# Three re-orderings in the dense half of an attention, MoE and MLP kernel: operand sums, an early load, and who copies the token numbers

## The chip, the cores and the metric

One core of a Trainium2 chip runs the whole program. The metric is the device time of one execution in microseconds; the kernel before takes 1034.37 us (median of 3 runs, 1034.16 to 1036.52). The engines are named as the profile names them: PE (matmul), DVE (vector), ACT (scalar), POOL (GpSimd), SP (issues most DMAs).

## The reference

```python
def _attn_ref(q, k, v):                        # 4 x 12 x 448 x 64
    scores = scale * np.matmul(q, k.transpose(0, 1, 3, 2)) - np.log(S)
    return np.matmul(1.0 / (1.0 + np.exp(-scores)), v)

def _moe_ref(x, w_gate, w1, w2):               # 1792 tokens x 768, 8 experts, F = 1024
    logits = x @ w_gate
    expert_idx = np.argmax(logits, axis=1)     # gate_w: softmax probability of that expert
    for e in range(E):
        mask = expert_idx == e
        h = np.maximum(x[mask] @ w1[e], 0.0)
        out[mask] = gate_w[mask, None] * (h @ w2[e])

def _moe2_ref(x, w_in, w_out):                 # 768 -> 2048 -> 768
    h = np.maximum(x @ w_in, 0.0)
    return h * h @ w_out
```

The output is `_moe2_ref(_moe_ref(attention))`, 1792 x 768 in float32.

## The kernel before

Three stages follow each other on one core. Attention fills about the first quarter of the span. Then the routed experts: tokens are sorted by expert and packed into 15 slots of 128 rows; each slot gathers its rows, multiplies through two weight matrices and writes its result rows to the DRAM table `y_d` (L587), whose 769th column is the token's number. Four "quarter" pieces of 32 rows take the overflow and are copied into `y_d` by POOL after the last slot (L803). A branch (L783) on the routing result skips six further slots.

The dense MLP, where the change lies, runs over two blocks of tokens: block 0 has two halves of 4 tiles of 128 tokens, block 1 two halves of 3 (`blocks`, P = 4 and 3). The two halves and the two halves of each weight matrix are combined in a Strassen-like scheme of seven products, so operands and weights have sums and differences formed on DVE.

- Every float32 matrix is split into a high and a low part: ACT copies it to the narrower type (`sh`, `wrh`), DVE subtracts to get the rest (`sl`, `wrl`). Each product is then three matmuls.
- `load_y` loads one tile of 128 rows of `y_d` to SBUF (`yn`, two buffers); `trans_y` has POOL copy its 769th column to `idx2` (L460, the row numbers for the final scatter), PE transpose it, and ACT and DVE split it.
- Layer 1: `layer1(c, h)` handles weight chunk c and token half h with 36 matmuls (two accumulations of 18); `steps` sets the order of the 16 calls of a block. Weight chunks pass through a ring of three; `advance` stages the next one.
- The weights of layer 2 are converted and summed by `narrow`. For five of the chunks (11 to 15) this is done in pieces between the matmuls of layer 1 in block 0: `rest()` is called four times per `layer1` and does one piece each time (40 pieces, of which some are empty). Sources lie in `rawb[2]`, results in `rawb[3]`; each chunk's result goes to the DRAM table `t_d` and comes back as `raw` when its turn comes (L416).
- Layer 2: seven products `o`, each of four steps `q`; g = 4*o + q counts the 28 steps of a block. A step has 6*P matmuls of 384 columns. `split_s(g + 2)` prepares the operand of the step two ahead. Products 0 to 6 read the operand blocks a11, a12, s2, s2 (after `a22 - s2`), a22, a11 (after `a11 + s2`), a12 (after `a12 - s2`), in this order. At the end of a product `evac` adds the PSUM tiles into the result (L914 on DVE, or ACT); products 2, 3 and 4 go on in the same PSUM tiles, so the first matmul of a product waits for the evacuation before it. After products 5 and 6 `scatter` writes result rows to `out` by an indirect DMA on POOL (L827).
- While block 0 is in steps g = 20 to 25 the six tiles of block 1 are loaded, transposed and split, one after each step.

Instructions of each engine run in the order in which the code was written (a manual schedule up to the last scatters), so an instruction that waits holds everything behind it on its engine. SP issues its DMAs in order too.

Of the kernel before, what the change touches and what calls it, by code (L numbers as in the profile page):

```python
# [40 lines left out]
QB = 2  # L41
# [20 lines left out]
def moe_kernel(ctx: ExitStack, tc: tile.TileContext, qk, v, wg, wm, w2, out):  # L62
# [363 lines left out]
    todo = [(n, k) for n in range(PRE, 16) for k in range(1, 9)]  # L426

    def rest():
        if not todo:
            return  # L430
        n, step = todo.pop(0)
        if step < 7:
            narrow(n, step, rawb[2], rawb[3], None)
        if step == 4 and n < 15:
            narrow(n + 1, 0, rawb[2], None, None)
        if step == 6:
            ready[0] = n + 1
            load_next()

    def load_y(bi, h, t, pool, bufs, tag="yn"):  # L440
        yn = pool.tile([128, DM + 1], F32, tag=tag, name=f"yn_{bi}_{h}_{t}", bufs=bufs)
        r_ = (blocks[bi][0] + h * blocks[bi][1] + t) * 128
        nc.sync.dma_start(out=yn, in_=y_d[r_:r_ + 128, :DM + 1])
        return yn
# [11 lines left out]
    def trans_y(bi, h, t, yn, yT, pool, tags):  # L456
        P = blocks[bi][1]
        n, yh, yl = yT
        c = blocks[bi][0] + h * P + t
        nc.gpsimd.tensor_copy(idx2[:, c:c + 1], yn[:, DM:].bitcast(U32))  # L460
        per = 3 if n == 3 else 4
# [20 lines left out]
    with ExitStack() as mctx:  # L482
# [250 lines left out]
        for s in range(NBASE):  # L733
            last = s == NBASE - 1
            up, down, fin = make_slot(s, *xs.pop(s), lambda c: (mh[c], ml[c]))
            if s + 2 < NBASE:
                regs(s + 2)
                if s > 0:
                    row0(s + 2)
                xg[s + 2] = gather(s + 2)  # L740
            for c in range(4):
                up(c)
# [40 lines left out]
        with tc.If(more < NT):  # L783
            for s in range(NBASE, NSLOT):
# [4 lines left out]
                def fresh(c, s=s, e_=e_):  # L789
                    wr = raw[6]  # L790
                    nc.gpsimd.dma_start(out=wr, in_=wm[ds(e_, 1), :, c].rearrange("a p n -> (a p) n"))
                    split_w(wr, mh[4 + c % 4], ml[4 + c % 4])
                    return mh[4 + c % 4], ml[4 + c % 4]
# [39 lines left out]
    load_next()  # L833
    yns = {t: load_y(0, 1, t, tp, 2) for t in range(2)}
    for bi, (t0, P) in enumerate(blocks):
# [7 lines left out]
        def layer1(c, h):  # L843
            w = used[0] + (0 if (c, h) not in ((1, 0), (7, 1)) or bi else 1)
            wc, wcl = wrh[w % RING], wrl[w % RING]
# [37 lines left out]
        if bi == 0:  # L883
            steps = [(0, 0), (1, 0), (0, 1), (1, 1)] + [(c, h) for c in range(2, 6) for h in range(2)] + [(6, 1), (7, 1), (6, 0), (7, 0)]
        else:
            steps = [(c, h) for c in range(8) for h in range(2)]
        seen = {}
        for c, h in steps:
            layer1(c, h)
            if bi == 0 and c < 2 and h == 0:  # L890
                for t in (2 * c, 2 * c + 1):
                    trans_y(0, 1, t, yns.pop(t), yT[1], ps_q, ("pq", "pq"))
                    if t + 2 < P:
                        yns[t + 2] = load_y(0, 1, t + 2, tp, 2)
            seen[c] = seen.get(c, 0) + 1
# [24 lines left out]
        def adds(o, q):  # L920
            a11, a12, s2, a22 = (hid[b, q][:, :2 * N] for b in range(4))
            if o == 1:
                V.tensor_tensor(a12, a12, s2, op=ALU.subtract)
            elif o == 2:
                V.tensor_tensor(a11, a11, s2, op=ALU.add)

        def third(g):
            o, q = divmod(g, 4)
            if o == 3:
                s2, a22 = hid[2, q][:, :2 * N], hid[3, q][:, :2 * N]  # L930
                V.tensor_tensor(s2, a22, s2, op=ALU.subtract)  # L931
# [6 lines left out]
        for o in range(len(PRODS)):  # L938
            for q in range(4):
                g = 4 * o + q  # L940
                third(g + 2)
                split_s(g + 2)
# [29 lines left out]
    order.close()  # L972
    prev = None
    for p in range(P):
        st = scatter(t0 + p, obs[0][p])
        if prev is not None:
            tc.declare_no_dep(st.ins, prev.ins, reason="every scatter writes rows of its own")
        prev = st

# [47 lines left out]
```

## Time and profile before

| | |
|---|---|
| median of 3 runs | 1034.37 us |
| the profiled execution | 1032.5 us, its span (first to last instruction) 1030.4 us |
| PE busy | 957.6 us, 93% of the span |
| DVE busy | 637.5 us, 62% |
| ACT busy | 566.3 us, 55% |
| POOL busy | 150.5 us, 15% |
| mean granted clock of PE | 0.967 of full speed |
| dense stage, from the first dense matmul to the end | 541.75 to 1030.4 us of the span |

The profile was taken on one execution, so its 1032.5 us is what durations add up to; it lies 1.9 us under the median of the runs. PE is the engine that sets the span, and its idle stretches are the time that can be had without taking work away. A stretch that PE passes at a granted clock near 0.5 (1.2 instead of 2.4 GHz) takes about twice its time at full speed.

### The profile page before, as it was taken

What the parts mean: (1) busy time and instruction counts of PE and PEld (TensorE: products, weight loads), DVE (VectorE), ACT (ScalarE), POOL (GpSimd) and SP (SyncE); (2) the same over time, 40 slices, a digit from 0 to 9 for tenths busy, and PEclk for the clock granted to TensorE, in tenths of its full rate; (3) what the DMA queues carried; (4) which work ended last, traced back from release to release, by engine and by line L of the source; (5) the groups of instructions that cost most, each with busy time, mean ns of one, the idle gap of its engine ahead of it and who ended that gap; (6) DMA issues with size and microseconds to landing.
All of it is one profiled execution on the core that took longest, in us unless ns stands there. A gap on an engine that the chain in (4) does not pass through costs nothing.

```text
span 1030.4 us, 15058 instructions
## 1 busy us (share of the span) xinstructions
PE 957.6 (93%) x5870; PEld 807.2 (78%) x5870; DVE 637.5 (62%) x657; ACT 566.3 (55%) x674; POOL 150.5 (15%) x134
## 2 busy tenths in 40 slices
PE   7999999288999999999996999999899699999896
PEld 3555555176888888888885788889899699999896
DVE  2877788688767767777754576236767322227762
ACT  4666666266777777777762444355344234446440
POOL 0000000237214323233211000000000110000002
PEclk9999999678999999999998999999999899999998
DMA  8789886633678594396555454303234431113202
GB/s 280 257 294 320 286 297 224 250 124 103 250 266 319 190 383 140 118 326 225 183 185 196 168 200 174 132 31 104 81 123 138 138 123 62 62 62 123 93 31 92
DMA packets 51261, 184.32 MB, mean 179 GB/s; under 512 B 7856, under 2 KB 18736, under 8 KB 49136
## 3 DMA queue, kind: packets, MB, share of 16 engines
q1 hardware_dynamic: 33136, 146.48, 40.4%
q0 software_dynamic: 6832, 31.07, 7.7%
q10 hardware_dynamic: 11216, 5.75, 2.2%
q8 instruction: 47, 0.77, 0.3%
q14 instruction: 30, 0.25, 0.1%
HBM read 209.62 MB, written 36.97 MB: 239 GB/s over the span
## 4 chain that ended last, share of the span: by engine, by line
PE 68%; DMA 4%; DVE 3%; issue 2%; ACT 2%; POOL 1%; POOLq 0%; SPq 0%; DVEq 0%; ACTq 0%
PE pp L854 7%; PE pp L853 7%; PE pp L855 7%; PE pq L958 6%; PE pq L959 6%; PE pq L960 6%; PE ph L523 4%; PE py L523 4%; PE py L525 4%; PE py L524 4%; PE ph L524 4%; PE ph L525 3%; DMA qraw<-in_wm 2%; PE qb L650 1%; DVE wl L397 1%
## 5 line engine op out<-in xcount | busy, mean ns | idle before, releaser
L397 DVE TENSOR_TENSOR wl<-raw,wh 128x1536 fp32r<-128x1536 f32 x103 | 202.9, 1978 | 70.6 <-ACT wh L396 67.9
L396 ACT ACTIVATE wh<-raw 128x1536 fp32r<-128x1536 f32 x120 | 177.8, 1488 | 14.7 <-DMA raw<-in_wm 7.0
L185 ACT ACTIVATE a<-sc,bias_s 128x896 f32<-128x896 f32 x96 | 82.5, 910 | 36.1 <-PE sc L181 36.0
L859 ACT ACTIVATE r<-pp 128x512 f32<-128x512 f32 (+1 forms) x64 | 34.8, 544 | 121.1 <-PE pp L855 121.1
L958 PE MATMUL pq<-wrh,sh 128*128 128x384 f32 x264 | 90.2, 342 | 4.2 <-DVE raw L914 4.2
L959 PE MATMUL pq<-wrl,sh 128*128 128x384 f32 x264 | 89.8, 340 | 0.0
L960 PE MATMUL pq<-wrh,sl 128*128 128x384 f32 x264 | 89.8, 340 | 0.0
L524 PE MATMUL py<-wl,hh 128*128 128x384 f32 x240 | 82.9, 346 | 5.2 <-POOL wl L397 5.2
L523 PE MATMUL py<-wh,hh 128*128 128x384 f32 x240 | 86.5, 360 | 0.0
L525 PE MATMUL py<-wh,hl 128*128 128x384 f32 x240 | 83.1, 346 | 2.4 <-DVE hl L553 2.4
L397 POOL TENSOR_TENSOR wl<-raw,wh 128x1536 fp32r<-128x1536 f32 x17 | 59.9, 3530 | 158.0 <-ACT wh L396 158.0
L397 DVE TENSOR_TENSOR wrl<-raw,wrh 128x1536 fp32r<-128x1536 f32 x30 | 52.8, 1759 | 38.4 <-ACT wrh L396 38.4
L523 PE MATMUL ph<-wh,xh 128*128 128x512 f32 x180 | 76.0, 422 | 0.3 <-ACT xh L509 0.3
L867 DVE TENSOR_TENSOR h<-h,h 128x512 f32<-128x512 f32 (+1 forms) x16 | 10.0, 625 | 102.0 <-ACT h L862 102.0
L879 ACT ACTIVATE sh<-h 128x1024 fp32r<-128x1024 f32 (+1 forms) x56 | 51.7, 944 | 38.1 <-DVE h L931 26.9
L524 PE MATMUL ph<-wl,xh 128*128 128x512 f32 x180 | 72.1, 401 | 0.0
L525 PE MATMUL ph<-wh,xl 128*128 128x512 f32 x180 | 72.0, 400 | 0.0
L880 DVE TENSOR_TENSOR sl<-h,sh 128x1024 fp32r<-128x1024 f32 (+1 forms) x56 | 59.8, 1087 | 17.8 <-ACT sh L879 17.7
L396 ACT ACTIVATE wrh<-raw 128x1536 fp32r<-128x1536 f32 x30 | 44.6, 1485 | 44.3 <-PE pq L960 36.1
L191 PE MATMUL po<-a,qkv 128*64 128x448 f32 x288 | 64.7, 556 | 0.0
L958 PEld LDWEIGHTS pq<-wrh,sh 128*128 128x128 f32 x264 | 50.6, 192 | 4.5 <-ACT rh L396 4.5
L853 PE MATMUL pp<-why,wrh 128*128 128x512 f32 (+1 forms) x132 | 49.6, 376 | 2.5 <-PEq L783 2.5
(232 smaller groups left out, 2169.7 us busy)
## 6 DMA issues: line engine op xcount, KB each, us to landing
raw<-in_wm SPq DMA_DIRECT2D x120, 768.0 KB
qraw<-in_wm SPq DMA_DIRECT2D x32, 768.0 KB
raw<-t_d SPq DMA_DIRECT2D x28, 768.0 KB
cs<-in_w SPq DMA_DIRECT2D x11, 1536.0 KB
raw<-w_d SPq DMA_DIRECT2D x16, 768.0 KB
qkv<-in_qk SPq DMA_DIRECT2D x23, 480.0 KB
raw<-in_w SPq DMA_DIRECT2D x5, 1536.0 KB
t_d<-raw POOLq DMA_DIRECT2D x5, 1536.0 KB, 7.1
```

What stands on the lines that cost most here:

```text
L185: nc.scalar.activation(a[:, :n], ps[:, :n, :S], AF.Sigmoid, bias=bias_s, scale=1.0 / math.sqrt(D))
L396: nc.scalar.activation(h, src, AF.Copy)
L397: (nc.gpsimd if pool else nc.vector).tensor_tensor(l, src, f32(h), op=ALU.subtract)
L523: nc.tensor.matmul(ps, lh, rh, start=first, stop=False)
L524: nc.tensor.matmul(ps, lh, rl, start=False, stop=False)
L525: nc.tensor.matmul(ps, ll, rh, start=False, stop=last)
L853: nc.tensor.matmul(pp[:, :N], lh, rh, start=(k == 0), stop=False)
L854: nc.tensor.matmul(pp[:, :N], lh, rl, start=False, stop=False)
L855: nc.tensor.matmul(pp[:, :N], ll, rh, start=False, stop=(k == KD - 1))
L958: nc.tensor.matmul(po[p][:, :DH], lh, wc[:, w0:w0 + DH], start=(q == 0 and kk == 0 and o in (0, 2, 5)), stop=False, **fl)
L959: nc.tensor.matmul(po[p][:, :DH], lh, wcl[:, w0:w0 + DH], start=False, stop=False, **fl)
L960: nc.tensor.matmul(po[p][:, :DH], ll, wc[:, w0:w0 + DH], start=False, stop=(q == 3 and kk == 1), **fl)
```

## The change

Three edits, and one on the branch that is not taken.

1. Operand sums. `a11 + s2` moves from the steps of product 2 to those of product 0; `a22 - s2` moves from `third(g + 2)`, called directly ahead of the split that reads it, to the steps of product 2, two steps ahead of that split. Each step of products 0, 1 and 2 then has one such sum, placed behind the step's split.
2. The second token half of block 0. Three of its four tiles are loaded in the last expert slot into `rawb[3]` (the result buffer of the weight conversion), the fourth after the branch as before. The pieces of the weight conversion are held for the first eight calls of `rest`. The order of `layer1` calls becomes three chunks of the first half, then three of the second.
3. The token numbers are copied to `idx2` by DVE instead of POOL. And the last three scatters are declared independent of each other in all pairs, not of the neighbour alone.

```diff
+    held = [8]
+
     def rest():
-        if not todo:
+        held[0] -= 1
+        if not todo or held[0] >= 0:
             return
...
     def load_y(bi, h, t, pool, bufs, tag="yn"):
-        yn = pool.tile([128, DM + 1], F32, tag=tag, name=f"yn_{bi}_{h}_{t}", bufs=bufs)
+        yn = pool if bufs is None else pool.tile([128, DM + 1], F32, tag=tag, name=f"yn_{bi}_{h}_{t}", bufs=bufs)
...
-        nc.gpsimd.tensor_copy(idx2[:, c:c + 1], yn[:, DM:].bitcast(U32))
+        nc.vector.tensor_copy(idx2[:, c:c + 1], yn[:, DM:].bitcast(U32))
...
+            if last:
+                yns = {t: load_y(0, 1, t, rawb[3][:, t * (DM + 1):(t + 1) * (DM + 1)], None) for t in range(3)}
...
                 def fresh(c, s=s, e_=e_):
-                    wr = raw[6]
+                    wr = mp.tile([128, CH], F32, tag="qraw", name=f"fr{s}_{c}", bufs=QB)
...
-    yns = {t: load_y(0, 1, t, tp, 2) for t in range(2)}
+    yns[3] = load_y(0, 1, 3, tp, 2)
...
-            w = used[0] + (0 if (c, h) not in ((1, 0), (7, 1)) or bi else 1)
+            w = bi * NW + c
...
-            steps = [(0, 0), (1, 0), (0, 1), (1, 1)] + [(c, h) for c in range(2, 6) for h in range(2)] + [(6, 1), (7, 1), (6, 0), (7, 0)]
+            steps = [(c, h) for h in range(2) for c in range(3)] + [(c, h) for c in range(3, 6) for h in range(2)] + [(6, 1), (7, 1), (6, 0), (7, 0)]
...
                     trans_y(0, 1, t, yns.pop(t), yT[1], ps_q, ("pq", "pq"))
-                    if t + 2 < P:
-                        yns[t + 2] = load_y(0, 1, t + 2, tp, 2)
...
         def adds(o, q):
             a11, a12, s2, a22 = (hid[b, q][:, :2 * N] for b in range(4))
-            if o == 1:
+            if o == 0:
+                V.tensor_tensor(a11, a11, s2, op=ALU.add)
+            elif o == 1:
                 V.tensor_tensor(a12, a12, s2, op=ALU.subtract)
             elif o == 2:
-                V.tensor_tensor(a11, a11, s2, op=ALU.add)
-
-        def third(g):
-            o, q = divmod(g, 4)
-            if o == 3:
-                s2, a22 = hid[2, q][:, :2 * N], hid[3, q][:, :2 * N]
                 V.tensor_tensor(s2, a22, s2, op=ALU.subtract)
...
-                third(g + 2)
                 split_s(g + 2)
...
-    prev = None
+    sent = []
     for p in range(P):
         st = scatter(t0 + p, obs[0][p])
-        if prev is not None:
-            tc.declare_no_dep(st.ins, prev.ins, reason="every scatter writes rows of its own")
-        prev = st
+        for other in sent:
+            tc.declare_no_dep(st.ins, other, reason="every scatter writes rows of its own")
+        sent.append(st.ins)
```

How this stands on the engines is shown at three places. First SP in the last expert slots, the kernel before: the DMAs from slot 13's loads to the branch (`y_d<-y` is a slot's result, `raw<-w_d` are weight chunks of layer 1, `raw<-in_w` a chunk for the conversion).

```order
L443 DMA yn_0_3_5088<-y_d 128x769
L95 DMA raw_1493<-in_w 128x3072
L587 ISA
L587 DMA y_d<-y_4952 128x769
L411 DMA raw_1367<-w_d 128x1536 x2
L587 ISA
L587 DMA y_d<-y_5126 128x769
```

The same place after the change:

```order
L446 DMA yn_0_3_5088<-y_d 128x769
L95 DMA raw_1493<-in_w 128x3072
L590 ISA
L590 DMA y_d<-y_4952 128x769
L446 DMA raw_1558<-y_d 128x769 x3
L411 DMA raw_1367<-w_d 128x1536 x2
L590 ISA
L590 DMA y_d<-y_5126 128x769
```

Three tile loads stand between the result of slot 13 and two weight loads; before, they stood behind the branch, after the result of slot 14 and the quarter copies.

Second, DVE in block 0, steps g = 10 and 11 of layer 2, up to the evacuation of product 2 (L914, later L917). Before (L397 is a weight chunk's low part, L931 `a22 - s2`, L925 `a11 + s2`, L880 the low part of a split):

```order
L397 TENSOR_TENSOR wrl_5195<-raw_1432,wrh_5194 128x1536
L931 TENSOR_TENSOR h_0_1_0_6606<-h_0_1_1_6632,h_0_1_0_6606 128x1024
L880 TENSOR_TENSOR sl_12_7624<-h_0_1_0_6606,sh_12_7623 128x1024
L925 TENSOR_TENSOR h_4_0_0_6927<-h_4_0_0_6927,h_4_1_0_6979 128x1024
L931 TENSOR_TENSOR h_2_1_0_6770<-h_2_1_1_6796,h_2_1_0_6770 128x1024
L880 TENSOR_TENSOR sl_13_7654<-h_2_1_0_6770,sh_13_7653 128x1024
L914 TENSOR_TENSOR raw_1493<-pq_2_0_7561,raw_1558 128x384
```

The same steps after the change (L930 is `a22 - s2`, L885 the low part):

```order
L397 TENSOR_TENSOR wrl_5198<-raw_1432,wrh_5197 128x1536
L885 TENSOR_TENSOR sl_12_7672<-h_0_1_0_6693,sh_12_7671 128x1024
L930 TENSOR_TENSOR h_4_1_0_7014<-h_4_1_1_7040,h_4_1_0_7014 128x1024
L885 TENSOR_TENSOR sl_13_7701<-h_2_1_0_6804,sh_13_7700 128x1024
L917 TENSOR_TENSOR raw_1493<-pq_2_0_7610,raw_1558 128x384
```

Two of the five operations between the weight chunk (L397) and the evacuation are gone, and no sum stands directly ahead of the split that reads it.

Third, POOL in the dense stage. Before:

```order
L460 COPY idx_80<-yn_1_3_6503 128x1
L125 DMA t_d<-raw_1558 128x8x384 x4
L460 COPY idx_80<-yn_0_0_7817 128x1
L460 COPY idx_80<-yn_0_1_7819 128x1
L460 COPY idx_80<-yn_0_2_7994 128x1
L827 DMA out<-raw_1558,idx_80 1792x768 x4
L460 COPY idx_80<-yn_1_0_8040 128x1
L460 COPY idx_80<-yn_1_1_8083 128x1
L460 COPY idx_80<-yn_1_2_8139 128x1
L827 DMA out<-raw_1493,idx_80 1792x768 x4
```

After:

```order
L808 DMA y_d<-yq_d 32x769
L125 DMA t_d<-raw_1558 128x8x384 x5
L832 DMA out<-raw_1558,idx_80 1792x768 x4
L832 DMA out<-raw_1493,idx_80 1792x768 x4
L832 DMA out<-raw_1558,idx_80 1792x768 x3
L832 DMA out<-raw_1493,idx_80 1792x768 x3
```

The copies of the last three tiles of block 1 stood behind the four scatters of product 5; POOL has only DMAs now, and each copy stands on DVE directly ahead of the low parts of its own tile.

## Rows read from the trace of the kernel before

**Rows 1.** Waits of PE, whole span (total us, times, longest).
```profile
PE pyt L466 <- DMA yn<-y_d: 15.7, 2, 8.5
PE pq L958 <- DVE raw L914: 8.0, 2, 4.2
```
**Rows 2.** PE in chosen stretches (busy us, instructions; granted clock; DMA share, GB/s).
```profile
559.00:563.80 4.80, 4.80 (x18) 0.52 0.97 375
696.00:720.00 24.00, 24.00 (x141) 1.00 0.30 99
744.60:747.90 3.30, 3.30 (x10) 0.50 0.00 0
969.60:973.10 3.50, 3.50 (x13) 0.52 0.02 5
```
**Rows 3.** Timeline of PE, dense start (start, us, work [idle before <-releaser]).
```profile
558.97 2.79 PE L466 MATMUL pyt<-ident,yn 128*128 128x128 f32 x12 [7.19 <-DMA yn<-y_d]
...
570.68 1.47 PE L466 MATMUL pyt<-ident,yn 128*128 128x128 f32 x12
573.89 0.50 PE L853 MATMUL pp<-hy,wrh 128*128 128x512 f32 x1 [1.74 <-ACT hy L470]
```
**Rows 4.** Timeline of SP, around the branch.
```profile
535.56 2.93 SPq L411 DMA_DIRECT2D raw<-w_d  x2
...
555.72 0.81 SPq L443 DMA_DIRECT2D yn<-y_d  x2
```
**Rows 5.** Timeline of POOL, last expert slot.
```profile
521.04 3.50 POOL L397 TENSOR_TENSOR wl<-raw,wh 128x1536 fp32r<-128x1536 f32 x1 [15.16 <-ACT wh L396]
```
**Rows 6.** Timeline of SP, then of ACT, end of layer 1, block 0.
```profile
645.30 42.15 SPq L416 DMA_DIRECT2D raw<-t_d  x5
...
683.84 1.48 ACT L396 ACTIVATE wrh<-raw 128x1536 fp32r<-128x1536 f32 x1
```
**Rows 7.** Timeline of all engines, block 0, products 2 to 3.
```profile
742.76 1.23 DVE L880 TENSOR_TENSOR sl<-h,sh 128x1024 fp32r<-128x1024 f32 x1 [1.20 <-ACT sh L879]
744.60 0.66 PE L958 MATMUL pq<-rh,sh 128*128 128x384 f32 x1 [3.86 <-DVE raw L914]
```
**Rows 8.** Timeline of DVE and PE, the same place in block 1.
```profile
961.74 0.95 DVE L931 TENSOR_TENSOR h<-h,h 128x768 f32<-128x768 f32 x1
968.23 1.48 DVE L914 TENSOR_TENSOR raw<-pq,raw 128x384 f32<-128x384 f32 x3
968.92 0.41 PE L958 MATMUL pq<-wrh,sh 128*128 128x384 f32 x1 [4.17 <-DVE raw L914]
```
**Rows 9.** Timeline of POOL, SP and PE, the last tile of block 1.
```profile
801.63 0.33 SPq L411 DMA_DIRECT2D raw<-w_d  x1
811.82 0.96 POOL L827 DMA_INDIRECT out<-raw,idx  x1 [2.92 <-DVE rl L397]
812.79 0.32 POOL L460 COPY idx<-yn 128x1 uint32<-128x1 uint32 x2
813.02 0.33 SPq L443 DMA_DIRECT2D yn<-y_d  x1
816.42 1.52 PE L466 MATMUL pyt<-ident,yn 128*128 128x128 f32 x6 [8.47 <-DMA yn<-y_d]
```
**Rows 10.** Timeline of SP and POOL, two tile loads right behind a weight load.
```profile
766.78 0.86 SPq L443 DMA_DIRECT2D yn<-y_d  x2
771.75 0.18 POOL L460 COPY idx<-yn 128x1 uint32<-128x1 uint32 x1 [131.91 <-DMA yn<-y_d]
```
**Rows 11.** Timeline of DVE and POOL, routing.
```profile
217.17 4.29 DVE L691 TENSOR_SCALAR cmq<-cmq 128x32 f32<-128x32 f32 x1
217.94 3.48 POOL L397 TENSOR_TENSOR wl<-raw,wh 128x1536 fp32r<-128x1536 f32 x1
221.49 0.18 DVE L692 TENSOR_REDUCE rq__1692<-cmq 128x4 f32<-128x32 f32 x1
```
**Rows 12.** Timeline of POOL, the last scatter.
```profile
1023.79 0.97 POOL L827 DMA_INDIRECT out<-raw,idx  x1 [1.60 <-DMA out<-raw,idx]
```

## The prediction

> **What bounds the kernel now.** The page first: PE is busy for 93% of the span, so time is won only where PE stands still or runs slowly, and the waits of PE name such places. I read that view next, for the dense stage alone, since the change lies there. Two groups stand out: transposes that wait for the load of a token tile (15.7 us in two waits) and second-layer matmuls that wait for an evacuation on DVE (8.0 us in two waits) [rows 1]. Then the timeline around each of the four, to see what was late: the wait's last releaser is only the end of a chain. Last the windows view, because each idle stretch is followed by a few microseconds in which PE was granted a clock of 0.50 to 0.52 against 1.00 in a steady stretch, that is 1.2 instead of 2.4 GHz [rows 2]. Half of such a stretch is lost time too, and goes if the idle stretch ahead of it goes.
>
> **The dense start.** Behind the first `layer1(0, 0)` PE wants tiles 0 and 1 of the second half and idles 7.19 us for them [rows 3]. Their loads left SP only at 555.72 [rows 4]: `y_d` is written at run-time addresses, so a load waits for every write issued ahead of it, the last slot's and the four quarter copies included. The changed kernel issues three of the four loads ahead of those writes. The result buffer they go to is last read by POOL's split, which starts at 521.04 and takes 3.50 [rows 5], so they leave SP near 525 and can be in place by about 530, 20 us early. They hold up two weight loads that left at 535.56 [rows 4]; that is their cover, 10 us of SP with nothing to issue. The fourth tile is loaded as late as before: issued at 555.72, there at 558.97 [rows 3, 4]. It is wanted only behind tile pieces 0 to 2 and `layer1(1, 0)`, which even with its slow start took from the end of the transposes at 561.8 to 570.68, over 8 us at full clock; counted from 551.78 (558.97 less the wait), that is 551.8 + 1.5 + 8 + 0.7, or 562. Three microseconds remain.
>
> The next wait is 1.74 us at 573.89, for the split of the last tiles directly ahead of `layer1(0, 1)` [rows 3]. With `layer1(2, 0)` put between, that split has 8 us. The chunks 0, 1 and 2 it uses are the whole ring and are staged before; chunk 3 is staged two calls (16 us) before its use. So this place gives 7.19 + 1.74 + half of the 4.8 slow us [rows 2, 3], together 11.3 us.
>
> **The held conversion** removes nothing and moves 40 pieces eight calls later, two `layer1` calls. Its DMAs move too: five source loads on SP, five writes to `t_d` on POOL, and the read-backs that SP has queued behind them. The first read-back that needs all five left at 645.30 and is used when the chunk is staged at 683.84 [rows 6]. Shifted, it leaves at 645.3 - 11.3 + 16.5 = 650.5, and the staging comes at 672.5: 22 us for one load. I cost this at nothing, with that as the cover. It ends at call 48 of 64, so it stays inside layer 1.
>
> **The operand sums.** Before the third product DVE does `a22 - s2`, idles 1.20 us for ACT's copy, does the low part (1.23), and so on twice, and only then comes to the evacuation for which PE has idled 3.86 us [rows 7]. Behind the change three operations stand between the weight chunk and the evacuation instead of five, and ACT's copies wait for nothing made directly ahead. Block 0, P = 4: a step is 24 matmuls at 0.17 us, 4.1 us [rows 2]; DVE has then a split and a sum of 1.2 us each, half a weight chunk and a quarter of the evacuation per step, 3.6 us in all, and the evacuation starts about a microsecond before PE needs it. The wait goes whole: 3.86 + half of 3.3 slow us, 5.5 us. Block 1, P = 3: a step is 18 matmuls, 3.1 us. DVE comes out of the weight chunk at 961.74 with three operations of 0.95 ahead of the evacuation's first 0.5 us (1.48 for three) [rows 8]: done at 965.1, or 0.1 to 0.2 us sooner where neighbours overlap. PE stopped at 968.92 - 4.17 = 964.75. So a wait of 0 to 0.4 us stays: 4.17 + 1.75 (half of 3.5 [rows 2]) - 0.4, 5.5 us. The four sums that move to product 0 in each block fall on steps with no other sum, like those of product 1, at which PE has no wait among rows 1; cost nothing, and if the cover fails 0.95 to 1.2 us each for the last.
>
> **The copies of token numbers.** PE idles 8.47 us for the last tile of block 1. Its load left at 813.02, when POOL had copied out of the buffer's former tile; that copy stood behind the scatter at 811.82 [rows 9]. On DVE the copy stands directly behind the weight chunk whose end also lets SP issue at 801.63 [rows 9]; the load follows at about 802. Two tile loads that left right behind a weight load at 766.78 had the first in place at 771.75, 5.0 us later [rows 10]; undisturbed the late one took 3.4 (813.02 to 816.42). So it arrives between 805.4 and 807, later if the scatters beside it cost something; PE asks at 807.95. I take 0.4 us of wait out of 0 to 1.5. Gain: 8.47 + 1.65 (the slow stretch behind it, as in block 0) - 0.4, 9.7 us. The fourteen copies themselves: on POOL two took 0.32 [rows 9]. On DVE no row shows this form; the ends are 0.16 (as on POOL, or 0.18 for a small operation [rows 11]) and 4.29, a 32-column operation beside a POOL one [rows 11]. I take 0.18, since POOL has only DMAs there. A DVE that is 62% busy hides that; at 4.29 the copy for the last tile would give back 4 us. Nothing below zero beyond the gain already counted, since POOL held nobody else.
>
> In rows 11 the DVE operation ends with POOL's, at 221.4. The Trainium skill's page SBUF — State Buffer (Who interferes with whom) says why: DVE and GpSimd share one pair of ports, and whoever has it locks the other out until its instruction ends. By that rule a copy that meets the issue of a scatter, 0.96 [rows 9], would come 1 us later and the sum be about 0.7 us smaller.
>
> **The last scatters.** The third waited 1.60 us for an earlier one's end [rows 12]. With all pairs independent only its issue is left, for which I leave 0.3: 1.3 us. The branch not taken adds nothing.
>
> **Sum.** 11.3 + 5.5 + 5.5 + 9.7 + 1.3 = 33.3 us. The profiled execution took 1032.5, of which 2.1 lie outside the span and stay: 999.2. It lay 1.9 us under the median of the runs, so the median should be 1001.
>
> **Rivals.**
> 1. The last tile stays late. For: its load is issued behind a weight load and beside the scatters; the margin is at most 2.5 us. Against: two loads of 0.4 and 0.8 MB in 5 us are about 230 GB/s, and 375 passed in one stretch [rows 2]. The page DMA: Bandwidth & Descriptors of the Trainium skill (Issuing engines are not separate DMA queues) says that DMAs of all issuers interleave on the same 16 engines; rows 10, without scatters, neither bear it out nor deny it. 4 us late gives 1001 + 5; the whole wait back gives 1011.
> 2. DVE stays last at the change from product 2 to 3. For: in block 1 it has no slack at all. Against: two operations and two waits for ACT are gone. One block back gives 1006.5, both 1012.
> 3. The change doesn't do what it says at the dense start: the early loads wait for the last writes after all. Against: they are issued ahead of those. Time 1012.
> 4. Slower. The held conversion ends too late and PE waits at step 2 of layer 2 for its second chunk. It decides once the read-back is more than 22 us later than I put it, and outweighs the rest beyond 22 + 33 = 55 us. For: its rounds are a chain of load, five DVE and ACT pieces, write and read-back, and SP holds them in order with tile and weight loads. Against: each round has the same eight calls as before and no tile load between. At 65 us late the time would be 1044.
>
> **How the numbers follow.** Forecast 0.72 (its own range 997 to 1005: no residual waits and 3 us for executions that differ as those of before did at the low end, both small waits at their ends and 2 us of new ones at the high); rival 1 0.11, rival 2 0.08, rival 3 0.04, rival 4 0.03, no net change from causes I don't see 0.02. The range, 996 to 1010, takes in the partial forms of rivals 1 and 2. A measurement here tells 0.3% (3 us) from nothing: faster 0.95, same 0.02, slower 0.03.
>
> **What would show it.** Right: no wait of PE for `yn` above 1.5 us, none for L917 above 0.5; no stretch at half clock near 560, 735, 800 and 950; the three early loads at 524 to 527 on SP; `layer1(2, 0)` directly behind the second pair of transposes; DVE reaching each evacuation of product 2 while PE is still in that product; a gap of about 1 us between the last scatters. Wrong: a wait of PE for weights (`rh`, `wrh`) early in layer 2 (rival 4), for `yn` near 800 (rival 1), for L917 (rival 2), or tile loads that leave after 540 (rival 3). Prediction and mechanism fail together if PE, with its idle gone, is granted less than full clock in the long stretches, which rows 2 give no sign of.

## The result, and the profile after

| | before | after |
|---|---|---|
| median, same chip | 1035.44 us (1034.16 to 1036.76, 4 runs) | 997.07 us (994.75 to 998.58, 4 runs) |
| profiled execution, its span | 1032.5, 1030.4 us | 997.18, 995.7 us |
| PE busy | 957.6 us, 93% | 948.8 us, 95% |
| DVE busy | 637.5 us | 637.6 us |
| mean granted clock of PE | 0.967 | 0.976 |

The ratio of the runs is 0.9627, 95% interval 0.9603 to 0.9652. In a later comparison on another chip it was 0.9644 (0.9620 to 0.9667), 996.59 against 1032.59 us. The forecast was 1001 us in a range of 996 to 1010. PE has 8.8 us less of busy time for the same matmuls: 7.4 us of that had been forecast as the half-clock stretches that go with the idle ones. One run below, of the kernel with the copies alone, took 1887.08 us where the other three took 1022.91 to 1026.3; it is left out there, and why it was slow no run shows.

First the waits of PE in the changed kernel, the view of [rows 1]. No wait for a token tile is left in it (no row has `pyt` or `yn`), and of the 8.0 us before an evacuation 0.3 remain. The largest wait of the dense stage is now the one at the branch ahead of it (3.0 us, 2.5 before), which the change doesn't touch.

```profile
PE pq L956 <- DVE raw L917: 0.3, 1, 0.3
```

To see where the time came from, the span is cut at places that both kernels pass. PE's timeline of before: the first dense matmul, layer 2 of block 0, the transposes of the fifth tile of block 1, layer 1 of block 1, its layer 2, the last matmul.

```profile
541.75 0.47 PE L853 MATMUL pp<-why,wrh 128*128 128x512 f32 x1 [2.49 <-PEq L783]
...
690.64 0.34 PE L958 MATMUL pq<-rh,sh 128*128 128x384 f32 x1
...
802.96 0.38 PE L466 MATMUL pyt<-ident,yn 128*128 128x128 f32 x2
...
827.04 0.33 PE L853 MATMUL pp<-why,wrh 128*128 128x384 f32 x1
...
927.13 0.34 PE L958 MATMUL pq<-wrh,sh 128*128 128x384 f32 x1
...
1020.32 0.34 PE L960 MATMUL pq<-wrh,sl 128*128 128x384 f32 x1
```

The same six places after the change:

```profile
541.37 0.47 PE L858 MATMUL pp<-why,wrh 128*128 128x512 f32 x1 [3.01 <-PEq L788]
...
678.36 0.34 PE L956 MATMUL pq<-rh,sh 128*128 128x384 f32 x1
...
785.05 0.41 PE L469 MATMUL pyt<-ident,yn 128*128 128x128 f32 x2
...
799.06 0.34 PE L858 MATMUL pp<-why,wrh 128*128 128x384 f32 x1
...
899.15 0.34 PE L956 MATMUL pq<-wrh,sh 128*128 128x384 f32 x1
...
986.89 0.34 PE L958 MATMUL pq<-wrh,sl 128*128 128x384 f32 x1
```

Differences of neighbouring starts give the stages, and the gain of each beside the term forecast for it:

| stage | before | after | gain | forecast |
|---|---|---|---|---|
| up to the dense start | 541.75 | 541.37 | 0.4 | 0 |
| dense start to layer 2 | 148.89 | 136.99 | 11.9 | 11.3 |
| layer 2 of block 0 to the fifth tile | 112.32 | 106.69 | 5.6 | 5.5 |
| fifth tile to layer 1 of block 1 | 24.08 | 14.01 | 10.1 | 9.7 |
| layer 1 of block 1 | 100.09 | 100.09 | 0 | 0 |
| layer 2 of block 1 | 93.19 | 87.74 | 5.4 | 5.5 |
| last matmul to the end of the span | 10.08 | 8.81 | 1.3 | 1.3 |
| sum | 1030.4 | 995.7 | 34.7 | 33.3 |

Now the four places. SP around the branch, the answer to [rows 4]:

```profile
521.37 0.35 SPq L590 DMA_DIRECT2D y_d<-y  x1
527.33 1.28 SPq L446 DMA_DIRECT2D raw<-y_d  x3
534.65 2.98 SPq L411 DMA_DIRECT2D raw<-w_d  x2
...
555.19 0.33 SPq L446 DMA_DIRECT2D yn<-y_d  x1
```

The three early loads leave 28 us ahead of the fourth and hold nobody: the weight loads behind them leave at 534.65 (535.56 before). PE then comes to its tiles at the dense start, the answer to [rows 3]; neither row has idle time ahead of it (early tiles have the name `raw`, their buffer's). `layer1(2, 0)`, still of the first half, follows at 561.97, and the first matmul of the second half at 570.45, both without idle time:

```profile
551.24 1.47 PE L469 MATMUL pyt<-ident,raw 128*128 128x128 f32 x12
...
561.40 0.82 PE L469 MATMUL pyt<-ident,yn 128*128 128x128 f32 x6
```

DVE and PE at the change from product 2 to 3 in block 1, the answer to [rows 8]. Behind the sum only one low part stands ahead of the evacuation, neither has waited for ACT, and PE loses 0.29 us instead of 4.17.

```profile
934.63 0.95 DVE L930 TENSOR_TENSOR h<-h,h 128x768 f32<-128x768 f32 x1
...
935.50 0.95 DVE L885 TENSOR_TENSOR sl<-h,sh 128x768 fp32r<-128x768 f32 x1
...
936.37 1.48 DVE L917 TENSOR_TENSOR raw<-pq,raw 128x384 f32<-128x384 f32 x3
...
937.06 0.41 PE L956 MATMUL pq<-wrh,sh 128*128 128x384 f32 x1 [0.29 <-DVE raw L917]
```

In block 0 the evacuation starts at 726.77, 1.5 us before PE leaves product 2, and no wait is recorded. The last tile of block 1, the answer to [rows 9], in a timeline of all engines:

```profile
783.60 0.15 DVE L463 COPY idx<-yn 128x1 uint32<-128x1 uint32 x1
783.61 0.99 POOL L832 DMA_INDIRECT out<-raw,idx  x1 [2.81 <-DMA out<-raw,idx]
...
784.14 0.37 SPq L446 DMA_DIRECT2D yn<-y_d  x1
...
790.05 0.85 PE L469 MATMUL pyt<-ident,yn 128*128 128x128 f32 x6
```

The copy ends 0.4 us before the load leaves, the load has 5.9 us, and PE finds the tile in place. Last, windows over the four places behind which PE ran at half clock before (columns as in [rows 2]): the dense start, the change from product 2 to 3 in block 0, the last tile of block 1, and the change from product 2 to 3 in block 1. Where [rows 2] has 0.50 to 0.52 (it doesn't show the third place) there is 1.00 now, 2.4 GHz.

```profile
559.00:563.80 4.80, 4.80 (x29) 1.00 0.01 3
...
727.00:731.00 4.00, 4.00 (x25) 1.00 0.01 2
787.00:800.00 13.00, 13.00 (x78) 1.00 0.55 200
935.00:945.00 10.00, 9.71 (x57) 1.00 0.45 152
```

### The profile page after: what moved, and what is told of

Read it like the earlier page. It is cut to its first block, busy times and chain, and to the rows that moved or that the text cites. A ratio compares the mean times of both kernels' runs of the same rounds, so it can differ in the third digit from the quotient of the medians.

```text
span 995.7 us, 15057 instructions
## 1 busy us (share of the span) xinstructions
PE 948.8 (95%) x5870; PEld 799.4 (80%) x5870; DVE 637.6 (64%) x671; ACT 565.8 (57%) x674; POOL 144.1 (14%) x120
## 5 line engine op out<-in xcount | busy, mean ns | idle before, releaser
L397 DVE TENSOR_TENSOR wl<-raw,wh 128x1536 fp32r<-128x1536 f32 x103 | 203.2, 1981 | 70.1 <-ACT wh L396 67.3
L397 POOL TENSOR_TENSOR wl<-raw,wh 128x1536 fp32r<-128x1536 f32 x17 | 60.0, 3534 | 161.4 <-ACT wh L396 161.4
L397 DVE TENSOR_TENSOR wrl<-raw,wrh 128x1536 fp32r<-128x1536 f32 x30 | 52.7, 1757 | 35.8 <-ACT wrh L396 35.8
L885 DVE TENSOR_TENSOR sl<-h,sh 128x1024 fp32r<-128x1024 f32 (+1 forms) x56 | 59.8, 1085 | 8.5 <-ACT sh L884 8.4
L832 POOL DMA_INDIRECT out<-raw,idx x14 | 13.7, 976 | 331.5 <-DVE raw L917 302.8
L884 ACT ACTIVATE sh<-h 128x1024 fp32r<-128x1024 f32 (+1 forms) x56 | 51.5, 943 | 13.5 <-PE pq L957 8.0
```

The lines of the kernel that those rows point to most:

```text
L397: (nc.gpsimd if pool else nc.vector).tensor_tensor(l, src, f32(h), op=ALU.subtract)
```

## The experiments

Three things had to be told apart: whether each part of the change earns what its stage shows, whether the mechanism inside each part is the one named, and how far away the slower outcome was. Stages below are those of the table above; a kernel's own execution is compared with that of the changed kernel (or of before), and a time with before on the same chip. A ratio is uncertain by 0.002 to 0.003, 2 to 3 us, and the median of before differed by 4 us between chips (1031.49 to 1035.44), so losses of a few microseconds are read from the stages, which agree to 0.3 us between kernels with the same waits at the same clock.

### Each part alone

Operand sums alone, in the kernel before:

```diff
         def adds(o, q):
-            if o == 1:
+            if o == 0:
+                V.tensor_tensor(a11, a11, s2, op=ALU.add)
+            elif o == 1:
...
             elif o == 2:
-                V.tensor_tensor(a11, a11, s2, op=ALU.add)
+                V.tensor_tensor(s2, a22, s2, op=ALU.subtract)
...
-                third(g + 2)
```

> The kernel before with the operand sums moved (a11 + s2 to product 0, a22 - s2 two steps ahead), nothing else. Theory (the four places are independent, each wait was the chain that the prediction named): the two waits of PE for L914 go but for 0 to 0.4 us in block 1, and the half-clock stretches behind them; both waits for yn stay at 7.2 and 8.5 us. Gain 11 us, ratio 0.989. Rival (the stages cover for each other, so that DVE's relief shows only once the loads are early): a gain under 6 us.

Measured: 1020.95 us, ratio 0.9863 (0.9844 to 0.9881). The waits of PE:

```profile
PE pyt L466 <- DMA yn<-y_d: 15.4, 2, 8.6
...
PE pq L953 <- DVE raw L914: 0.3, 1, 0.3
```

Both waits for tiles stay, and of the two for the evacuation 0.3 us are left. The two layer-2 stages gain 5.6 and 5.4 us, as in the whole change. The profiled execution is 10.6 us shorter than that of before, near the 11 us expected; by the ratio it is 14.2 us, with 12.3 as its lower end, more than was expected.

The early loads, the held conversion and the order of `layer1` alone:

```diff
+    held = [8]
...
+            if last:
+                yns = {t: load_y(0, 1, t, rawb[3][:, t * (DM + 1):(t + 1) * (DM + 1)], None) for t in range(3)}
...
-            steps = [(0, 0), (1, 0), (0, 1), (1, 1)] + [(c, h) for c in range(2, 6) for h in range(2)] + [(6, 1), (7, 1), (6, 0), (7, 0)]
+            steps = [(c, h) for h in range(2) for c in range(3)] + [(c, h) for c in range(3, 6) for h in range(2)] + [(6, 1), (7, 1), (6, 0), (7, 0)]
```

> The kernel before with the three early loads, the held conversion and the new order of layer1 calls; token numbers still copied by POOL, sums as before. Theory: the wait of 7.2 us at the dense start and the 1.7 us behind it go with their slow stretch, 11.3 to 11.9 us gained, ratio 0.9888; the 8.5 us wait near 800 and the two L914 waits stay. Rival (POOL's copies, which now stand behind the conversion's writes, hold a tile): a wait for yn comes back at the dense start, gain under 8.

Measured: 1021.1 us, ratio 0.9881 (0.9853 to 0.9909).

```profile
PE pyt L469 <- DMA yn<-y_d: 8.7, 1, 8.7
```

One of the two tile waits is left, that of the last tile of block 1; the waits for evacuations are the 8.0 us of before. From the dense start to layer 2 it takes 135.39 us, 13.5 less than before and 1.6 less than the whole change takes there (the last section says what differs). The later stages are within 0.2 us of before.

The copies on DVE alone:

```diff
-        nc.gpsimd.tensor_copy(idx2[:, c:c + 1], yn[:, DM:].bitcast(U32))
+        nc.vector.tensor_copy(idx2[:, c:c + 1], yn[:, DM:].bitcast(U32))
```

> The kernel before with the token numbers copied by DVE, nothing else. Theory (the tile load waited for POOL's copy behind a scatter): the last load of block 1 leaves right behind the weight load, at about 802, and PE's 8.5 us wait goes with its slow stretch: 9.7 to 10.1 us, ratio 0.9905; the 7.2 us wait at the dense start stays as it is. Rival (the load is late by SP's order and by traffic): it leaves about 802 but lands late, and half the wait stays: 5 us.

Measured: 1023.58 us, ratio 0.9888 (0.9866 to 0.9911).

```profile
PE pyt L466 <- DMA yn<-y_d: 8.0, 1, 8.0
```

Here it is the dense start's wait that is left, again beside 8.0 us for evacuations. The stage of the last tile gains 10.2 us, as in the whole change (10.1). But the two layer-2 stages take 1.2 and 1.0 us longer than before with the same waits; the last section shows by what.

Taken from the ratios the three are worth 14.2, 12.3 and 11.6 us, each within 2 to 3; with 1.3 for the scatters that is 39.4, against 38.6 for the whole by its ratio. If they share a gain, it is less than the noise of that sum, some 4 us. The stages say it more sharply, since each part alone gains in its own stage what the whole change gains there: four separate stalls on one engine in sequence.

### The mechanism inside each part

The early loads taken out of the change, its order of work kept:

```diff
-            if last:
-                yns = {t: load_y(0, 1, t, rawb[3][:, t * (DM + 1):(t + 1) * (DM + 1)], None) for t in range(3)}
...
-    yns[3] = load_y(0, 1, 3, tp, 2)
+    yns = {t: load_y(0, 1, t, tp, 2) for t in range(2)}
...
+                    if t + 2 < P:
+                        yns[t + 2] = load_y(0, 1, t + 2, tp, 2)
```

> The changed kernel with the second half's tiles loaded behind the branch again, two and two, in the new order of layer1 calls. Theory (early load and order do two different things): the 7.2 us wait for tiles 0 and 1 is back with 2.4 us of half clock, the 1.7 us wait for the split is not: 9.6 us slower than the changed kernel, about 28 to 29 us faster than the kernel before. Rival (the order alone hides the load): within 3 us of the changed kernel.

Measured: 1005.88 us, ratio 0.9724 (0.9706 to 0.9741). The timeline of PE at the dense start:

```profile
556.90 2.79 PE L469 MATMUL pyt<-ident,yn 128*128 128x128 f32 x12 [8.12 <-DMA yn<-y_d]
```

The wait for tiles is back, the 1.74 us of [rows 3] is not, and the stage takes 145.08 us, 8.1 more than in the changed kernel. That kernel passed part of the stage at a lower clock (last section) and this one did not; beside the 135.4 us of kernels that did not either it is 9.7, where 9.6 had been expected. The opposite edit, loads early and the order of before:

```diff
-            steps = [(c, h) for h in range(2) for c in range(3)] + [(c, h) for c in range(3, 6) for h in range(2)] + [(6, 1), (7, 1), (6, 0), (7, 0)]
+            steps = [(0, 0), (1, 0), (0, 1), (1, 1)] + [(c, h) for c in range(2, 6) for h in range(2)] + [(6, 1), (7, 1), (6, 0), (7, 0)]
```

> The changed kernel with the former order of layer1 calls in block 0 (two chunks of the first half, then the second half), the loads early. Theory: PE waits 1.7 us for the split of the last tiles ahead of layer1(0, 1) and loses some 0.4 more in the two matmuls behind it: 2 us slower, no other wait. Rival (the fourth tile, still loaded behind the branch, is what the new order hides): a wait for yn of several us, 5 us or more slower.

Measured: 999.14 us, ratio 0.9688 (0.9672 to 0.9704). PE's timeline at that place:

```profile
562.89 0.50 PE L858 MATMUL pp<-hy,wrh 128*128 128x512 f32 x1 [1.74 <-ACT hy L473]
```

The wait for the split is back to the hundredth and the wait for tiles stays away; the stage takes 139.43, 2.4 more. Loads and order each remove one wait, as the prediction had divided them.

For the sums: is it the chain (a sum directly ahead of the split that reads it, so ACT and DVE wait for each other) or only the number of operations of DVE ahead of the evacuation? First `a22 - s2` back directly ahead of its split, with `a11 + s2` left at product 0:

```diff
-            elif o == 2:
+
+        def third(g):
+            o, q = divmod(g, 4)
+            if o == 3:
+                s2, a22 = hid[2, q][:, :2 * N], hid[3, q][:, :2 * N]
                 V.tensor_tensor(s2, a22, s2, op=ALU.subtract)
...
+                third(g + 2)
```

> The changed kernel with a22 - s2 put back directly ahead of the split that reads it; a11 + s2 stays in product 0. Theory (what made DVE late was the chain sum, ACT's copy, low part, twice in a row, with DVE idle for ACT): the waits of PE for the evacuation of product 2 come back at 2.5 to 2.7 us in block 0 and about 3.3 in block 1, with a half-clock stretch of 1.6 us lost behind each: 8 to 9 us slower than the changed kernel, about 1006. Rival (it was the number of sums in the steps of product 2, halved here too): no wait above 1 us, within 2 us of the changed kernel.

Measured: 1004.88 us, ratio 0.9739 (0.9714 to 0.9764). All engines, block 1, products 2 to 3:

```profile
940.56 0.84 ACT L884 ACTIVATE sh<-h 128x768 fp32r<-128x768 f32 x1 [1.97 <-DVE h L934]
...
941.43 0.96 DVE L885 TENSOR_TENSOR sl<-h,sh 128x768 fp32r<-128x768 f32 x1 [0.99 <-ACT sh L884]
...
943.01 0.66 PE L961 MATMUL pq<-wrh,sh 128*128 128x384 f32 x1 [3.30 <-DVE raw L917]
```

ACT's copy waits for the sum (L934), DVE's low part waits for ACT, and PE for the evacuation behind them: 2.73 us in block 0 (a row of the same form at 731.15) and 3.30 here. The two layer-2 stages lose 3.0 and 5.8 us, 8.7 of the 11.1 that the sums gained. The counterpart: `a22 - s2` two steps ahead, but `a11 + s2` beside it in product 2, so two sums per step and no chain:

```diff
-            if o == 0:
-                V.tensor_tensor(a11, a11, s2, op=ALU.add)
-            elif o == 1:
+            if o == 1:
...
+                V.tensor_tensor(a11, a11, s2, op=ALU.add)
```

> The changed kernel with both sums in each step of product 2 (a11 + s2, then a22 - s2 two steps ahead of its split) and none in product 0. Theory (the chain decides, not the number): no wait in block 0 beyond 0.5 us, and in block 1, where DVE has no slack, 1 to 1.5 us without a long half-clock stretch: 1 to 3 us slower than the changed kernel. Rival (the number decides): waits near 4 us in both blocks again, 10 us slower.

Measured: 1000.95 us, ratio 0.9705 (0.9689 to 0.9722). All engines, the same place:

```profile
936.16 0.96 DVE L929 TENSOR_TENSOR h<-h,h 128x768 f32<-128x768 f32 x1
...
938.61 0.41 PE L955 MATMUL pq<-wrh,sh 128*128 128x384 f32 x1 [2.55 <-DVE raw L917]
```

No wait stands on DVE's rows, and still the evacuation comes late: PE waits 1.05 us in block 0 and 2.55 in block 1, the stages lose 1.3 and 4.0 us. Both accounts hold, each for a part. In block 0, where a step of PE is 4.1 us, the chain decides (2.73 us of wait against 1.05). In block 1, at 3.1 us a step, the number of sums weighs nearly as much (3.30 against 2.55). The expectation for two sums was too low in both blocks (0 to 0.5 and 1 to 1.5 us of wait).

The place of the copies in POOL's queue, tested inside the change:

```diff
-        nc.vector.tensor_copy(idx2[:, c:c + 1], yn[:, DM:].bitcast(U32))
+        nc.gpsimd.tensor_copy(idx2[:, c:c + 1], yn[:, DM:].bitcast(U32))
```

> The changed kernel, but the token numbers copied by POOL as before. Theory (the place in POOL's queue, behind the scatters, is what held the last tile's load): PE waits 8 to 9 us for the last tile of block 1, 9 to 10.5 us more than the changed kernel with the half-clock stretch; the other tiles as in the changed kernel. Rival (with the sums moved, the stretch of SP and POOL is different and the last load would have been in time anyway): 0 to 3 us more.

Measured: 1007.22 us, ratio 0.9753 (0.9732 to 0.9774), beside 996.59 for the changed kernel on that chip: 10.6 us more. All engines, the last tile of block 1:

```profile
791.96 0.96 POOL L832 DMA_INDIRECT out<-raw,idx  x1 [3.27 <-issue]
792.92 0.32 POOL L463 COPY idx<-yn 128x1 uint32<-128x1 uint32 x2
793.15 0.33 SPq L446 DMA_DIRECT2D yn<-y_d  x1
...
796.53 1.51 PE L469 MATMUL pyt<-ident,yn 128*128 128x128 f32 x6 [9.63 <-DMA yn<-y_d]
```

It is [rows 9] again: scatter, copies, load, PE. The copy itself takes 0.15 us on DVE and 0.18 on POOL (two in 0.32); what it costs is the place in the queue, through the buffer that it keeps.

### How near the slower outcome was

The prediction's fourth rival was a conversion held too long. It was held for 20 calls, and in a later comparison for 16, instead of 8:

```diff
-    held = [8]
+    held = [20]
```

> The changed kernel with the weight conversion held for 20 calls instead of 8, three layer1 calls more. The read-back that needs all five conversions then leaves 25 us later, at 675.6 instead of 650.8, and is there at about 679.5; its staging stood at 671.5. Theory as predicted (it decides at step 2 of layer 2, which is 8 us behind the start at 678.4): a wait of 0 to 3 us. Rival (ACT, which runs in order, waits for the read-back at 671.5 and holds the evacuations of layer 1 and the first operand splits behind it): PE idles 5 to 7 us ahead of layer 2 and loses 1 to 2 more at half clock, 6 to 9 us slower.

Measured: 1006.72 us, ratio 0.9754 (0.9733 to 0.9774). From the timelines of SP, ACT and PE, the end of layer 1 in block 0:

```profile
680.27 13.38 SPq L416 DMA_DIRECT2D raw<-t_d  x6
...
684.46 1.48 ACT L396 ACTIVATE wrh<-raw 128x1536 fp32r<-128x1536 f32 x1 [8.79 <-DMA raw<-t_d]
...
686.95 0.69 PE L956 MATMUL pq<-rh,sh 128*128 128x384 f32 x1 [4.41 <-ACT sh L884]
```

The read-back leaves 29.5 us later than in the changed kernel (650.80, the line below), where 25 had been expected. ACT stands 8.79 us at the staging copy, and what PE misses at the start of layer 2 is not that weight but the operand copy `sh` queued behind it on ACT. Ahead of that PE waits twice in layer 1, 1.44 and 1.03 us, for an `r` of ACT; there ACT stood at a piece of the conversion itself (L109), 6.19 and 5.84 us, for DVE. The two stages around it lose 7.9 and 3.5 us.

```profile
650.80 48.40 SPq L416 DMA_DIRECT2D raw<-t_d  x8
```

> The changed kernel with the pieces of the weight conversion held for sixteen calls, not eight, so two more layer1 calls (16.5 us) later. By the prediction's arithmetic the first read-back leaves at 650.8 + 16.5 = 667.3 and its chunk is staged at 671.6, 4.3 us for a load that takes about 5: a wait of 1 to 2 us, 1 to 3 us in all. Rival (cover of that arithmetic is wrong, since ACT's pieces hold its other work as at twenty calls, which cost 11 us): 5 to 8 us.

(The same line with `held = [16]`.) Measured: 995.15 us, ratio 0.9637 (0.9611 to 0.9663). ACT at that place (the read-back left at 666.49):

```profile
670.65 1.49 ACT L396 ACTIVATE wrh<-raw 128x1536 fp32r<-128x1536 f32 x1 [0.52 <-DMA raw<-t_d]
```

15.7 us later, ACT waits 0.52 us, and PE hardly at all (0.3 us for an `r` of ACT). No loss can be told in the times, where 1 to 3 us were expected. So the cover is about 15 us (15.7 less 0.52), and at 29.5 us the delay costs 11 us of stages.

### A further edit

In the first expert slots PE waits 3.6 us for POOL, in the kernel before as well as after. The changed kernel, all engines:

```profile
233.20 6.89 POOL L397 TENSOR_TENSOR wl<-raw,wh 128x1536 fp32r<-128x1536 f32 x2
...
234.97 6.75 DVE L397 TENSOR_TENSOR wl<-raw,wh 128x1536 fp32r<-128x1536 f32 x1 [1.50 <-ACT wh L396]
...
236.74 0.69 PE L527 MATMUL py<-wl,hh 128*128 128x384 f32 x1 [3.61 <-POOL wl L397]
```

One of the two POOL operations was given to DVE, and the changed kernel run once more beside it:

```diff
-                split_w(raw[c], mh[c], ml[c], pool=(c in (4, 7)))
+                split_w(raw[c], mh[c], ml[c], pool=(c == 4))
```

> The changed kernel with the low part of one of the first slot's weight chunks (chunk 7) formed on DVE instead of POOL. In the changed kernel POOL's two such operations took 6.89 us from 233.20 beside one of DVE that took 6.75 us from 234.97, and PE waited 3.61 us for them and ran at half clock behind. If that is the two engines excluding each other: the two on DVE take 1.8 us each, PE's wait at 236.7 falls to 0 to 1.5 us, 2 to 4 us off the changed kernel (ratio to it 0.996 to 0.998). Rival (DVE is the late one whoever does it, since it now has one operation more): PE waits 2 to 4 us for DVE's low part, no difference or up to 2 us slower.

> The changed kernel once more, as the base for the three beside it: ratio to before 0.963 (0.960 to 0.966), span 995 to 997 us, no wait of PE for yn and none over 0.5 us for an evacuation of product 2.

Measured: 995.33 us (992.0 to 995.78), ratio to before 0.9629 (0.9608 to 0.9651); the changed kernel 996.59 (993.4 to 998.66), 0.9644 (0.9620 to 0.9667). DVE there:

```profile
232.39 1.75 DVE L397 TENSOR_TENSOR wl<-raw,wh 128x1536 fp32r<-128x1536 f32 x1
```

The operation takes 1.75 us, and PE's wait at 236.7 is gone. The first dense matmul comes at 536.94 us, where the thirteen other profiled executions have it between 539.58 and 542.77, the two of the changed kernel at 541.37 and 540.83. So the place gains 3.9 to 4.4 us in the traces, the upper end of the 2 to 4 expected; in the times the two intervals overlap, and whether this kernel beats the changed one is not settled.

## Why the prediction was right

**The reading.** Each of the four waits was traced back one step further than its last releaser, to what kept that releaser: writes ahead of a load, an operation order on DVE, a copy that keeps a buffer. Undoing three of these inside the change brought the whole wait back (8.12, 1.74 and 9.63 us for 7.19, 1.74 and 8.47). For the evacuations the order of sum and split alone brought back 2.73 of 3.86 us and 3.30 of 4.17, and the number of sums alone 1.05 and 2.55.

**The dense start.** 11.3 forecast, 11.9 measured. The 0.6 us more fit the order of calls, put at its wait of 1.74: undoing it cost 2.4. The early loads left at 527.33, not near 525: the result of slot 13 went out ahead of them only at 521.37, and SP waits 5.6 us there for that write, while the prediction, which names this rule for the late loads, had timed the early ones by their buffer alone. 24 us from there to their use made that harmless. The fourth tile was there for its transposes at 561.40; the 3 us of margin held.

**The sums.** 5.5 and 5.5 forecast, 5.6 and 5.4 measured. The wait left in block 1 is 0.29 us, within the 0 to 0.4 given. The reasons were the right two, with the weights that the two experiments gave. A step's work on DVE in block 0 adds up to 3.8 us and not 3.6 (1.22 for a split, 1.22 for a sum, half of 1.75, a quarter of 1.95), still less than PE's 4.1; the evacuation came 1.5 us early where about 1 was put.

**The copies.** 9.7 forecast, 10.1 measured: the 0.4 us that was set aside for a late tile wasn't needed. PE asked for the tile at 790.05, 5.9 us behind the load's issue, and the load's own time, 3.4 to 5.0 by the rows, fitted in. The fourteen copies took 0.14 to 0.15 us each. The rival that a copy which meets a scatter is held up, 0.7 us less in the sum, was not borne out: the copy at 783.60 met a scatter at 783.61, took 0.15, and the scatter 0.99 us. The Trainium skill's page SBUF — State Buffer (Who interferes with whom), which the prediction drew on for it, has the lock for DVE instructions with two inputs in SBUF or in a two-port mode, and says that one with at most one SBUF input outside those modes does not contend with GpSimd. The prediction had left that condition out; the copy has one input, and the trace agrees with the page if it ran outside those modes, which no run shows.

**The last scatters.** 1.3 forecast and measured; the gaps on POOL are 0.30 and 0.31 us, where 1.60 stood in [rows 12]. The profiled executions without this edit end 10.1 us behind the last matmul, all those with it 8.8.

**The held conversion.** Forecast for the first read-back 650.5, for its staging 672.5; measured 650.80 and 671.55. Cost nothing, as put. The rival built on it was mis-described: the 22 us of cover forgot the load's own 4.2 us and took the staging 1 us too late (about 15 were there), and the place is not step 2 of layer 2 but its first step, through operand copies that stand behind the staging on ACT, and layer 1 before it.

**Where luck helped.** The half-clock stretches were sized by one execution of before, and the gains were measured against the same one. In the kernel with the copies alone the two in layer 2 lasted over 5.5 us, not 3.3 and 3.5 (last section), so a term can differ by a microsecond with the mechanism as put. That the terms agree within 0.6 us is partly luck.

**The mis-sized step.** The median came 3.9 us under the forecast. Half of that is the terms: the profiled execution took 997.18 where the sum gave 999.2 (1.4 us in the stages, 0.6 outside the span, 1.5 now and 2.1 before). The other 1.9 is the last line of the sum, "It lay 1.9 us under the median of the runs, so the median should be 1001". The profiled execution of before lay below all three runs shown with it (spans on another chip ran from 1028.7 to 1034.9 in nine runs, against 1030.4 in the profile); that of the changed kernel lay 0.1 above its median. The offset of one execution did not carry to another kernel. What before's other executions spend those 2 us on is open, since only one of them was profiled; longer half-clock stretches are a candidate that no run tests.

## What to carry to other kernels

Follow an idle stretch of the bounding engine back past its last releaser until something is found that could have been issued earlier or elsewhere, and count the half-clock stretch behind it as well, with a range, since its length differs between executions: here that was put at 7.4 of the 33.3 us. A one-element operation is priced by what stands ahead of it in its engine's queue and by what it keeps from being released, not by its 0.15 us. Do not transfer the offset between one profiled execution and the median from one kernel to the next; put it into the range.

## What the runs showed of the hardware

**Two clocks at the dense start.** Behind the branch PE is granted less than full clock in some kernels' executions and not in others. Windows of the changed kernel, and of the one held for 16 calls:

```profile
541.50:551.00 9.50, 9.50 (x35) 0.82 0.39 126
```

```profile
541.50:551.00 9.50, 9.50 (x50) 1.00 0.37 119
```

A mean of 0.82 is a part at 1.2 GHz and the rest at 2.4. Both kernels have an idle stretch of 2.7 to 3.0 us just ahead, and the same matmuls from there on. The stage to layer 2 takes 137.0 us with the one and 135.4 with the other (135.39 with the early loads alone, 135.38 with two sums, 135.91 here). The execution with the late loads has 1.00 in this window too, so its stage is to be set beside the 135.4 (its wait for tiles falls into the window's end, hence the 7.28 us busy):

```profile
541.50:551.00 9.50, 7.28 (x33) 1.00 0.37 118
```

In the kernel before this made little difference, since PE then waited for tiles anyway; with the wait gone 1.6 us of an execution hang on it. What decides it no run here shows.

**The same wait, half-clock stretches of different length.** In layer 2 of the kernel with the copies alone PE waits 3.86 and 4.17 us, to the hundredth as in the kernel before ([rows 7], [rows 8]). Behind these waits before ran 3.3 and 3.5 us at half clock ([rows 2]), this kernel more than 5.5 both times:

```profile
747.10:752.60 5.50, 5.50 (x17) 0.50 0.12 19
962.40:967.90 5.50, 5.50 (x17) 0.50 0.24 62
```

The two stages took 113.47 and 94.19 us for 112.32 and 93.19. With the sum back at its split, the 2.73 us of wait in block 0 were followed by no such stretch (the stage lost 3.0 us). So what an idle stretch costs beyond itself was anything from nothing to 2.8 us here, and one execution doesn't size it.

**DVE and POOL hold each other up.** The 128x1536 low part of a weight chunk takes DVE 1.75 us by itself and 6.75 beside POOL's two, which took 6.89 together (one alone 3.50 in [rows 5]). In the last experiment it happened again one slot later, 4.62 us beside a POOL operation of 4.33. The Trainium skill's page SBUF — State Buffer (Who interferes with whom) has it that a DVE instruction with two inputs in SBUF contends with a GpSimd instruction that reads SBUF; the trace agrees with these numbers. DVE loses 5.0 us that way; the two operations that POOL has would take it 3.5.
